# Mask rows of q and k: one ScalarE operation over 128 PSUM rows instead of two over 64, with the sign of q turned

## The chip, the cores and the metric

The kernel runs on one core of a Trainium2 chip. The metric is the device time of one execution in microseconds (us); a version's time is the median of several runs. Five engines work side by side: TensorE (PE), VectorE (DVE), ScalarE (ACT), GpSimd (POOL) and SyncE (SP), which here only issues DMA transfers. Each takes its instructions in a fixed order.

## What is computed

The reference is an attention in which a query sees only the keys of its own cluster, followed by a gated convolution. With B = 4, H = 8, S = 768, D = 64 and 16 centroids for each head:

```python
q_assign = argmax(q_n @ c_n.T)          # cluster of each query, normalised vectors
k_assign = argmax(k_n @ c_n.T)
mask     = q_assign[..., :, None] == k_assign[..., None, :]
scores   = where(mask, q @ k.T / 8, -1e9)
x        = softmax(scores) @ v          # heads side by side: [4, 768, 512]
x1, x2, x3 = split(x @ w_proj, 3)       # w_proj: 512 x 1536
conv     = irfft(rfft(x2, n=768) * rfft(filter_fft, n=768), n=768)   # along the sequence
out      = (x1 * conv * x3) @ w_out     # [4, 768, 512] float32
```

## The kernel before, in words

The work is cut into eight groups n of four heads, half a batch each, and a group into two pairs of heads (pr). The code doesn't issue its work where it stands: `build` describes operations, each with the engines that could do it, what it reads and writes, and a planned time. A table, ORDER, then says for all of them in which order they are issued, on which engine (P, A, V, G, S for the five engines) and in which of the eight PSUM banks. So the order on each engine is that of the table, and an operation that waits holds back what the table put behind it on its engine.

`routing(n)` prepares a group. q and k come into SBUF (`qkraw`, DMAs of L286 on SyncE), are transposed (L560 on VectorE for n of 2 and more) into `qkT` (`qkP` in the trace), and cast to bf16 into `augs` (L249 where ScalarE does it, L251 where GpSimd or VectorE does): 64 rows of q or k for each head of a pair. The similarity to the centroids (L589, TensorE) is turned (L594), its maximum found and compared (L602, L603), and the one-hot choice turned back (`ohT`). One more product (`bank<-ohT,tri` of L71) leaves in a PSUM bank, for 384 positions, 16 rows for each head: those of q on PSUM rows 0 to 63, those of k on rows 64 to 127. Two banks hold the 768 positions. ScalarE brings them to `oh2`, a bf16 view of 64 rows of the tile `sim` with q's and k's 768 values side by side: L612 for q (a copy with scale BIG and bias −BIG), L617 for k (Relu). That makes four operations a routing, 64x384 each, for n = 1 to 7. `masks` (L491) then copies 16 rows for each head with a SyncE DMA into `aug2`, right beside the 64 cast rows, q's and k's 768 values in one transfer: four transfers a routing. The first group (n = 0) has its own way, `first_masks`, which writes the mask rows straight from PSUM (L534 on VectorE, L537 on ScalarE).

`attention(n, pr)` then takes, for each of six key tiles, the scores as a product of 80 or 128 rows (`bank<-aug` of L71), in which the mask rows add nothing for a key of the same cluster and a large negative number for the others. ScalarE exponentiates them with scale 0.125 (L657, L660) into one of five `p` buffers, TensorE multiplies by v (L671, `pair<-p,vraw`), and VectorE (L692) and GpSimd (L688) add up the denominators. Three slots of `augs` go round (`ring`). After each second group the batch's hyena part follows: projection (L809 and others), spectrum (L478), products (L833, L837, L923), output.

The helper `product` (L69, L71) issues most matmuls, and `copy` (L249, L251) most copies and casts, so in the profile these lines stand for several places of the program, and the tile names tell them apart.

Of the kernel before, what the change touches and what calls it, by code (L numbers as in the profile page):

```python
# [14 lines left out]
F32 = mybir.dt.float32  # L15
# [111 lines left out]
P0:7 A30 G12 A43 S42 V16 V31 S44 S41 A45 G25 P1:6 P2:7 P3:6 A34 V49 V50 V32 G29 P4:7 G20 P5:6 P6:7 P7:6 S48 S47 P8:7  # L127
A46 G11 P9:6 P10:7 P70:7 G17 V33 A35 P72:6 S126 S125 V51 G13 G14 G24 A36 A53 V37 P38:5 A71 P66:4 V55 V56 A73 V57 G19
P64:3 A67 V39 P78:4 S124 G28 A65 P76:3 V40 S123 P99:5 V52 A59 A54 V58 V15 G18 A62 A60 A63 P101:6 A102 S130 A100 V21
G61 P146:7 A147 P144:2 P95:1 S129 P93:0 S127 A96 P252:5 V79 A94 P254:7 P151:1 G22 A69 A98 V77 V80 V145 V81 V82 S128  # L130
G23 P88:0 A89 V104 V74 S132 V75 A253 A255 P83:6 V84 S293 V85 A153 S291 P105:2 S122 G154 G68 P107:3 P248:4 P246:5 V90
V108 P148:7 V106 V92 A249 P185:3 A247 A186 P140:4 V141 G103 P264:2 A265 V149 V152 S289 P218:5 A219 P266:4 P192:3
P258:2 A193 S298 A267 G26 G27 G256 P260:5 G97 A259 S136 G250 V87 V91 V86 P212:6 P189:4 A261 V109 A190 P187:3 A188
P194:2 A195 P222:0 A223 S299 V110 A213 V111 P270:15 S290 P117:2 A118 G199 P112:3 A115 P202:0 V150 G200 P196:7 P210:4
A211 P204:6 G139 S295 A197 V272 V271 V273 V274 G135 G201 V121 A203 V113 G138 V275 S294 P206:1 A207 A205 V209 P191:45
A119 P214:0 S292 A120 A116 G134 S297 S133 P226:1 A227 A114 S137 S300 A215 S286 P198 P220:2 A221 P279:6 P228:7 A229
V268 P306:1 A307 P276:3 A277 P304:0 A305 V217 S131 P230:2 A231 V225 P208 P311:1 A312 V317 P309:7 P313:0 G363 V233 A278
A263 P216 V157 V156 A281 S301 S296 S287 S288 A314 P224 A280 S283 S282 V159 P335:3 A257 P302:0 A303 P321:6 A322 P337:1
A310 V316 V433 S245 S464 S465 P232 A234 P235:6 G158 V236 S237 G155 A338 P319:7 A320 A269 P327:0 P323:2 S284 V439 A262
V436 A324 P308:45 S285 P329:7 A251 V430 S460 S461 S468 P331:6 A332 P315 A328 G318 P347:2 A348 V326 V162 P339:1 P325  # L140
P345:2 S471 P371:0 S463 A330 A340 A346 P369:7 A336 A370 V334 A372 A435 V160 V342 S462 P373:6 A374 S458 S238 P343:1
A344 A432 S459 P388:2 P333 A389 P378:0 A379 S362 P442:37 P380:6 V444 A434 S469 P376:1 A377 V350 P341 P398:0 A399 A381
P349 A351 V443 A431 G163 P386:1 P394:0 S473 A387 P352:7 A353 P396:6 A397 P390:3 A391 P406:2 A407 V445 V446 V447 G383
P375:45 P474:7 V719 P414:6 P448:1 A449 G385 S470 S466 A395 A450 A415 P382 A475 S354 P451:2 A453 A452 V239 S240 G368
V716 V384 S467 P412:0 S454 P478:3 A479 V164 S355 P410:1 A411 A413 S242 P392 S241 P404:7 P481:2 S457 S455 V393 A482
V161 V401 A405 P402:6 A403 V409 P400 P166:0 A167 P483:2 A484 P165:7 A169 A171 P503:6 P408 A504 V417 V172 S748 V170
P485:2 A486 P476:1 A477 G489 S745 P416 V356 P142:2 A418 A441 G437 P174:6 V143 S472 P419:1 A420 S357 S421 S422 A175
V168 V243 V244 P495:3 A438 V722 P173:0 A177 V178 P493:2 A494 V176 G364 A440 V725 G365 P491:1 P480:45 P487 P499:2 S456
G488 G490 A496 A492 V498 P515:6 A500 P509:7 P511:3 A510 S358 P501:0 A502 V506 P653:1 A512 P497 V423 P507:0 A654 S747
A508 P664:7 A665 P517:3 A518 A516 P505 P674:7 A675 P672:0 V514 P660:1 P519:3 A520 V522 P657:2 P513 S359 V360 A673  # L150
P678:3 A661 P662:0 S752 V361 S424 A658 A663 S754 S429 P655:7 A656 A721 G667 P728:61 V729 A679 V730 V731 P524:7 S534
S425 V732 P180:0 A525 A717 A720 S526 P521 G669 A523 P670:6 A671 P686:1 A687 V181 V733 V668 S426 P179:7 P682:3 A183
P688:2 A689 V182 S527 V528 S529 P659:45 P666 A683 P734:3 A735 G367 V427 P698:2 A699 P764:7 A765 A736 P676 V677 V428
P680:2 P690:7 S530 A681 V685 P694:3 A695 P696:1 A697 P769:6 P760:2 A761 A691 P684 P737:2 A738 P762:1 A739 S531 A763
V693 G366 A770 A727 P779:3 A780 P692 P700 A702 V701 G703 P793:6 P767:1 A768 V532 P785:3 V533 P777:2 A778 V774 P771:7
A772 G776 S746 V184 A718 P766:45 S744 V886 P535:2 P537:7 A536 V538 P787:0 A786 G775 V539 G704 P781:2 A782 V784 S756
P545:1 P789:3 A546 A790 S759 A788 V792 P540:2 A541 P542:1 V543 S755 P795:0 A796 S753 P547:3 V548 P801:2 A726 P773 V544
P783 S749 A724 S740 S741 P825:1 S758 P844:0 V549 A794 A723 V892 P797:3 A798 A826 P832:6 A833 P803:7 S743 A804 S757
P791 V895 S751 G551 S750 G553 P805:1 G705 S822 S742 V800 P799 P830:7 V889 A806 A802 A845 A890 A831 P842:2 S927 P850:1
P898:60 P834:7 S715 V808 A851 S914 P852:3 A843 V550 S706 G810 P823:1 G552 V900 V899 V901 S915 A853 V902 G838 P807 A824  # L160
P554:1 V555 A809 P827:6 A828 P858:0 V556 A835 G839 P557:3 V558 P578:2 A579 P848:6 A849 P840:7 G811 A859 A841 P829:45
S929 G812 V559 P836 V903 S916 V837 S707 A887 V847 A888 V561 S921 P860:7 P947:3 A861 S924 P930:0 A931 S926 P904:6 A905
S918 A906 P856:1 A857 P868:2 A869 P934:7 A935 P846 P939:6 A940 S917 P907:0 A908 S885 P562:1 A909 V855 P854 A948 S919
V863 V564 V708 P864:6 A865 P565:7 V567 P937:0 A938 V709 A891 P866:2 A867 G560 V563 S920 S911 P593:3 A594 V566 P959:6
P951:0 A952 G569 V871 G873 A897 V568 P862 P870 P932:1 P582:7 V1174 P570:0 A872 V571 A933 V572 P949:3 P973:2 S922 A583
P584:1 V585 P941:7 A942 S813 G945 V1177 A950 P936:45 A974 S710 A960 P573:7 V575 V574 G946 G944 P967:3 A968 V954 P955:0
S923 P963:2 A964 V577 P975:1 A976 A956 P1115:6 P943 P957:1 A958 V962 S925 P953 P965:1 G874 G875 A966 A1176 A1116 S910
P1120:0 P1138:7 P1118:2 A1119 P971:3 P1132:1 S711 P961 A893 P1128:6 A1129 V576 A972 V970 S814 A1121 P969 V978 A896
G980 P586:26 S1209 A587 V589 V588 G590 P1130:3 A1133 P597:0 A894 A1131 S1204 S712 P977 S928 A1179 V1183 S1208 S912
P580:1 V581 P599:6 V1180 P601:23 A1139 A598 V600 G591 A602 V604 V603 P1140:1 A1141 P1136:7 A1137 V815 V816 P595:0 V596  # L170
G592 P1122:1 A1123 S1202 P1146:6 A1147 P1111:7 A1112 P1186:23 G981 V713 V714 P1148:7 A1149 P612:0 P608:6 S913 A979
V1187 V1188 V1189 S876 G1125 V1127 S1203 P1113:7 A613 A1114 V1126 P1220:1 G982 P616:23 V605 S1207 P1154:0 V1135 S817
P1117:45 V1190 S1205 V606 S877 A609 V878 V879 P1152:6 A1153 P1144:7 A1184 S992 S819 P1124 A1178 P1134 A1221 P1142 A617
V619 A1155 A1145 V618 G607 V1191 S818 P1229:0 P614:7 V615 G620 A1230 P1218:3 P1227:2 S1211 A1228 A1219 P1150 P1156:2
A1157 V820 P1237:3 V1143 P1247:7 P1222:0 A1223 S1217 P1192:1 A1193 A1194 P1235:6 A1236 V821 S880 P1158 V1151 P1225:0
S983 P610:1 A1160 A1226 V1234 P1195:6 A1196 V1159 P625:2 S1206 P1224:45 S984 V985 V986 G621 S881 A1197 V611 V622 A1248
A1238 P1243:6 P1245:7 A1244 A1246 S882 V883 S1198 V884 P623:0 A624 V626 P1253:3 A1254 P627:6 S1199 P1263:7 S987 A1264
A628 A1175 P631:01 A632 P1239:3 A1240 G1161 P1261:7 V1347 P1231 G1233 P629:6 V630 P1251:3 A1252 V634 A1262 G1232 S989
P1241 A1181 V633 V1242 S988 S1210 G1162 S1216 G1163 P1255:3 V1250 P1259:7 P1285:1 V990 A1185 P1290:0 V991 A1256 V1258
P1288:6 A1289 A1291 A1260 V635 P1249 P1298:3 A1299 P1283:2 A1284 V1266 G1268 P1316:6 G636 P1257 P1302:7 A1303 P1281:3  # L180
A1282 G637 P1310:0 P1003:2 P993:7 A994 P995:3 V996 S1201 V997 P1000:7 A1311 S1213 P1005:0 A1004 S1212 V1006 V1007
A1286 P998:1 A999 A1182 P1265 A1317 V1001 S1173 G1009 G1008 P1292:0 P1314:1 A1315 P1036:3 A1267 P1040:6 V1350 S1377
P1308:1 A1309 A1041 S1215 A1037 P638:2 V1002 A1293 A639 S1214 V1353 P1051:7 A1052 V1344 V1010 P1055:6 S1164 V1011
# [48 lines left out]
def build(T):  # L232
# [249 lines left out]
    def oh2():  # L482
        return T.sim[:64].rearrange("p a b -> p (a b)").bitcast(BF16).rearrange("p (j s) -> p j s", j=2)
# [59 lines left out]
    def routing(n):  # L543
# [64 lines left out]
        for ch in range(2):  # L608
# [7 lines left out]
            def relu(e, ch=ch, h=h):  # L616
                T.nc.scalar.activation(oh2()[:, 1, ts(ch, 384)], ap(h)[64:, :384], Act.Relu)  # L617
# [342 lines left out]
    def constants():  # L960
# [35 lines left out]
        def small(e):  # L996
            G().memset(T.half_pi, math.pi / 2)
# [227 lines left out]
```

## Time and profile before

| | |
|---|---|
| median of 3 runs | 355.24 us (354.19, 355.83, 355.24) |
| the profiled execution's own time | 353.72 us |
| its span, first to last instruction | 352.0 us |
| granted TensorE clock, mean | 0.997 |
| TensorE busy | 339.8 us, 97% |
| VectorE busy | 324.9 us, 92% |
| ScalarE busy | 275.8 us, 78% |
| GpSimd busy | 155.4 us, 44% |
| evictions to `oh2`, L612 and L617 | 14 each, 0.484 and 0.487 us at the median |
| mask transfers, L491 | 28, issue 0.548 us at the median |

In the profile a row such as `L671 PE MATMUL pair<-p,vraw 128*64 128x385 f32 x768` names the line, the engine, the operation, the tile written and those read, the shape and the number of instructions. SPq and PEq are the sequencers of SyncE and TensorE. An engine's busy time is the union of its instructions' times. A matmul counts from its start to its modelled end, and the next one may start before that. "idle before" is what an engine stood still ahead of the row's operations, with the operation or transfer whose end let it go on.

### The profile page before, as it was taken

What the parts mean: (1) busy time and instruction counts of PE and PEld (TensorE: products, weight loads), DVE (VectorE), ACT (ScalarE), POOL (GpSimd) and SP (SyncE); (2) the same over time, 40 slices, a digit from 0 to 9 for tenths busy, and PEclk for the clock granted to TensorE, in tenths of its full rate; (3) what the DMA queues carried; (4) which work ended last, traced back from release to release, by engine and by line L of the source; (5) the groups of instructions that cost most, each with busy time, mean ns of one, the idle gap of its engine ahead of it and who ended that gap; (6) DMA issues with size and microseconds to landing.
All of it is one profiled execution on the core that took longest, in us unless ns stands there. A gap on an engine that the chain in (4) does not pass through costs nothing.

```text
span 352.0 us, 8375 instructions
## 1 busy us (share of the span) xinstructions
PE 339.8 (97%) x3174; PEld 222.8 (63%) x3176; DVE 324.9 (92%) x452; ACT 275.8 (78%) x513; POOL 155.4 (44%) x175
## 2 busy tenths in 40 slices
PE   7889999999999999999999999999999999999994
PEld 3445445465656568766787577866887865567672
DVE  7999899899999999999989999999988999989993
ACT  5999999999998998887987796869886564534332
POOL 7678405142134545373336638372433054147610
PEclk9999999999999999999999999999999999999998
DMA  8999666875698998998696868983467353310134
GB/s 173 224 161 211 124 103 106 154 153 159 104 175 142 157 173 119 126 124 149 115 194 87 125 80 159 184 161 76 67 141 80 88 156 110 107 61 0 57 126 181
DMA packets 126324, 45.69 MB, mean 130 GB/s; under 512 B 113720, under 2 KB 118604, under 8 KB 126284
## 3 DMA queue, kind: packets, MB, share of 16 engines
q1 hardware_dynamic: 120396, 34.12, 49.0%
q0 software_dynamic: 2960, 9.77, 19.2%
q10 hardware_dynamic: 2928, 1.28, 1.4%
q8 instruction: 25, 0.41, 0.5%
q14 instruction: 15, 0.12, 0.2%
HBM read 31.59 MB, written 7.40 MB: 111 GB/s over the span
## 4 chain that ended last, share of the span: by engine, by line
PE 75%; ACT 3%; DVE 0%; issue 0%; ACTq 0%; DVEq 0%
PE bank L71 38%; PE pair L671 27%; PE bank L809 6%; PE bank L589 2%; PE bank L478 1%; ACT aug L249 1%; ACT p L657 1%; PE bank L705 1%; ACT p L660 0%; PE bank L762 0%; ACT tm L450 0%; PE bank L69 0%; DVE tm L833 0%; ACT tm L249 0%; DVE x L875 0%
## 5 line engine op out<-in xcount | busy, mean ns | idle before, releaser
L671 PE MATMUL pair<-p,vraw 128*64 128x385 f32 x768 | 141.7, 487 | 0.5 <-issue 0.5
L660 ACT ACTIVATE p<-bank 128x512 f32<-128x512 f32 x192 | 108.4, 601 | 27.4 <-PE bank L71 22.1
L692 DVE TENSOR_TENSOR acc<-p,acc 128x1536 f32<-128x1536 f32 x64 | 112.1, 1751 | 4.5 <-ACT p L660 2.1
L71 PE MATMUL bank<-aug 80*64 80x512 bf16 (+3 forms) x746 | 91.7, 330 | 2.3 <-ACT p L660 1.2
L671 PEld LDWEIGHTS pair<-p,vraw 128*64 128x64 f32 x768 | 66.7, 137 | 36.6 <-issue 23.6
L71 PEld LDWEIGHTS <-aug 80*64 80x64 bf16 (+1 forms) x746 | 66.1, 152 | 32.2 <-issue 20.4
L688 POOL TENSOR_TENSOR acc<-p,p 128x512 f32<-128x512 f32 x33 | 42.4, 1312 | 41.9 <-DVE xT L772 22.7
L657 ACT ACTIVATE p<-bank 128x512 f32<-128x512 f32 x96 | 56.2, 602 | 2.9 <-PE bank L71 2.1
L725 POOL DMA_DIRECT2D acc<-acc x30 | 24.4, 814 | 72.9 <-DMA acc<-acc 32.5
L71 PE MATMUL bank<-xT,wpj 128*64 128x384 bf16 x504 | 49.8, 326 | 0.0
L249 ACT CAST aug<-qkP 64x768 bf16<-64x768 f32 x52 | 42.7, 829 | 1.1 <-DVE qkP L560 0.3
L71 PEld LDWEIGHTS <-wpj 128*64 128x64 bf16 x504 | 33.8, 110 | 11.6 <-issue 2.8
L71 PEld LDWEIGHTS <-y 128*64 128x64 bf16 x504 | 27.0, 110 | 10.2 <-issue 2.1
L923 POOL TENSOR_TENSOR y<-yy,x 128x768 bf16<-128x768 f32 x11 | 20.1, 1825 | 24.0 <-DVE yy L911 23.7
L833 DVE TENSOR_TENSOR tm<-bank,hm 128x512 f32<-128x512 f32 x44 | 28.1, 678 | 1.4 <-PE bank L478 0.9
L560 DVE STREAM_TRANSPOSE qkP<-qkraw 128x768 f32<-128x768 f32 x24 | 22.7, 960 | 1.8 <-ACT aug L249 0.9
L71 PE MATMUL bank<-wout,y 128*64 128x512 bf16 (+1 forms) x200 | 23.9, 371 | 0.0
L837 POOL TENSOR_TENSOR y<-tm 128x512 bf16<-128x512 f32 x15 | 19.9, 1352 | 6.7 <-DVE tm L833 2.9
L809 PE MATMUL bank<-wpj,xT 128*64 128x512 bf16 x192 | 22.3, 379 | 0.0
L249 ACT COPY ob<-bank 128x512 f32<-128x512 f32 x20 | 11.6, 587 | 9.4 <-PE bank L71 8.0
L772 DVE SCALAR_TENSOR_TENSOR xT<-osb,rb 128x384 bf16<-128x384 f32 x30 | 17.4, 609 | 0.7 <-DMA rb<-dr 0.7
L809 PEld LDWEIGHTS <-xT 128*64 128x64 bf16 x192 | 13.3, 110 | 6.8 <-issue 0.4
(160 smaller groups left out, 402.9 us busy)
## 6 DMA issues: line engine op xcount, KB each, us to landing
vraw<-in_v_dram SPq DMA_DIRECT2D x16, 384.0 KB
rb<-dr SPq DMA_DIRECT2D x30, 192.0 KB
qkraw<-in_k_dram SPq DMA_DIRECT2D x48, 96.0 KB
qkraw<-in_q_dram SPq DMA_DIRECT2D x48, 96.0 KB
out_dram<-ob SPq DMA_DIRECT2D x9, 512.0 KB
acc<-acc POOLq DMA_DIRECT2D x10, 384.0 KB, 6.1
acc<-acc POOLq DMA_DIRECT2D x10, 192.0 KB, 4.3
wpj<-in_moe_w_proj_dram POOLq DMA_DIRECT2D x4, 384.0 KB, 5.3
```

The costliest lines, as they stand in the source:

```text
L71: T.nc.tensor.matmul(out[64 * i:64 * i + 64], lhsT[:, 64 * i:64 * i + 64], rhs, start=start, stop=stop)
L249: T.nc.scalar.copy(out, in_)
L560: op(("DVE", .9), lambda e, s=s, j=j, pr=pr: V().transpose(T.qkP[pr][:, S * j:S * j + S], T.qkraw[s][:].rearrange("p t h d -> p (t h d)")) ...
L657: T.nc.scalar.activation(o, ap(h).rearrange("p (a b) -> p a b", a=2), Act.Exp, scale=0.125)
L660: T.nc.scalar.activation(flat(s)[:, lo:lo + 512], ap(h), Act.Exp, scale=0.125)
L671: T.nc.tensor.matmul(o[64 * hp:64 * hp + 64, ch, :385], T.vraw[vs][:, hp, sk * D:(sk + 1) * D], T.p[slots[sk]][:, hp, 384 * ch:384 * ch + ...
L688: alu(e).tensor_tensor(o, x, y, op=Alu.add)
L692: T.nc.vector.tensor_tensor(T.acc[os], T.p[slots[sk]][:, :, :S], T.acc[os], op=Alu.add)
L725: op(("POOL", .8), lambda e, rows=rows: T.nc.gpsimd.dma_start(flat_()[:rows], flat_()[rows:2 * rows], accum_op=Alu.add), te, r=[], w=AK, b ...
L809: T.nc.tensor.matmul(ap(h)[64 * i:64 * i + 64], T.xT[xs][:, kt, tokens(m, i, w_)], T.wpj[:, kt, DM:2 * DM], start=kt == 0, stop=kt == ND - 1)
L833: op(("DVE", .68), lambda e, i=i, cs=cs, r=r, h=h: T.nc.vector.tensor_tensor(T.tm[r][:, cs], ap(h), hmrow(i, (0, 2, 2, 3)[2 * r + cs]), op ...
L923: op(("DVE", .95) if last else {"DVE": .95, "POOL": 1.85}, lambda e, dt=dt, x3=x3, yy=yy: alu(e).tensor_tensor(T.y2[:, dt], yy().rearrange ...
```

## The change

For n = 1 to 7 one ScalarE operation now takes all 128 PSUM rows of a bank, q's and k's alike: Relu(scale · x + bias), with scale and bias from a new tile `rank` of one number for each row, 1 and 0 for k's rows and −BIG and BIG for q's. Two operations of 128x384 stand for four of 64x384. Relu leaves only values of zero or more, so q's mask rows come out with the opposite sign (BIG − BIG·x where −BIG + BIG·x was). So the q casts multiply by −1 and the exponential's scale becomes −0.125; the first group's constants are turned to match. `oh2` now keeps q on rows 0 to 63 and k on rows 64 to 127, 768 values each, so a mask transfer takes either q's or k's 16 rows: 56 transfers of 16x768 for 28 of 16x1536. `rank` is filled by four GpSimd memsets near the program's start.

```diff
-P0:7 A30 G12 A43 S42 V16 V31 S44 S41 A45 G25 P1:6 P2:7 P3:6 A34 V49 V50 V32 G29 P4:7 G20 P5:6 P6:7 P7:6 S48 S47 P8:7
+P0:7 A31 G12 A44 S43 V16 V32 S45 S42 A46 G26 P1:6 P2:7 P3:6 A35 V50 V51 V33 G30 P4:7 G21 P5:6 P6:7 P7:6 S49 S48 P8:7
...
     def oh2():
-        return T.sim[:64].rearrange("p a b -> p (a b)").bitcast(BF16).rearrange("p (j s) -> p j s", j=2)
+        return T.sim[:].rearrange("p a b -> p (a b)").bitcast(BF16)[:, :S]
...
-                out.append(op(("SP", .6), lambda e, a=a, hp=hp, lo=lo: dma(e)(
-                    T.aug2[a][hp][64 - 64 * hp:80 - 64 * hp], oh2()[lo:lo + NC]),
...
+                for j in range(2):
+                    out.append(op(("SP", .6), lambda e, a=a, hp=hp, lo=lo, j=j: dma(e)(
+                        T.augs[a][hp][j][64 - 64 * hp:80 - 64 * hp], oh2()[64 * j + lo:64 * j + lo + NC]),
...
-                            T.nc.scalar.activation(o, x, Act.Relu if j else Act.Copy, scale=1.0 if j else BIG,
-                                                   bias=0.0 if j else -BIG)
+                            T.nc.scalar.activation(o, x, Act.Relu if j else Act.Copy, scale=1.0 if j else -BIG,
+                                                   bias=0.0 if j else BIG)
...
+                        if j:
+                            copy(e, o, x)
+                        elif e == "ACT":
+                            T.nc.scalar.activation(o, x, Act.Copy, scale=-1.0)
+                        else:
+                            alu(e).tensor_scalar(o, x, -1.0, None, op0=Alu.mult)
...
-            op(("ACT", .44), lambda e, ch=ch, h=h: T.nc.scalar.activation(
-                oh2()[:, 0, ts(ch, 384)], ap(h)[:64, :384], Act.Copy, scale=BIG, bias=-BIG), due, r=[h],
-               w=[("oh2", 0)] + (SIM if not ch else []), free=[h])
-
-            def relu(e, ch=ch, h=h):
-                T.nc.scalar.activation(oh2()[:, 1, ts(ch, 384)], ap(h)[64:, :384], Act.Relu)
-            op(("ACT", .44), relu, due, r=[h] + ([("oh2", 0)] if not ch else []), w=[("oh2", 1)], free=[h])
+            def ranks(e, ch=ch, h=h):
+                T.nc.scalar.activation(oh2()[:, ts(ch, 384)], ap(h)[:, :384], Act.Relu, scale=T.rank[:, 0:1], bias=T.rank[:, 1:2])
+            op(("ACT", .49), ranks, due, r=[h, "rank"], w=[("oh2", ch)] + (SIM if not ch else []), free=[h])
...
-                        T.nc.scalar.activation(flat(s)[:, lo:lo + 512], ap(h), Act.Exp, scale=0.125)
+                        T.nc.scalar.activation(flat(s)[:, lo:lo + 512], ap(h), Act.Exp, scale=-0.125)
...
+        def rank(e):
+            G().memset(T.rank[:, 0:1], 1.0)
+            G().memset(T.rank[:, 1:2], 0.0)
+            G().memset(T.rank[:64, 0:1], -BIG)
+            G().memset(T.rank[:64, 1:2], BIG)
+        op(("POOL", .4), rank, 7, w=["rank"])
```

ORDER is numbered anew, since there are fewer ScalarE operations and more transfers; the lines above show its first row of both versions. On TensorE, VectorE and GpSimd the remaining operations keep their order. What moves is on ScalarE and SyncE.

On ScalarE at the routing n = 2 (about 58 to 63 us in the trace of before), the first whose evictions stand among exponentials, before: `bank_66` and `bank_67` are the two PSUM banks with the mask rows, `sim` is where `oh2` lies, the `p` tiles are the exponentials' results, `aug` those of the casts.

```order
L660 ACTIVATE p_99<-bank_64 128x512
L612 ACTIVATE sim<-bank_66 64x384
L657 ACTIVATE p_99<-bank_63 128x2x256
L660 ACTIVATE p_98<-bank_65 128x512
L657 ACTIVATE p_100<-bank_64 128x2x256
L617 ACTIVATE sim<-bank_66 64x384
L249 CAST aug_93<-qkP_109 64x768
L617 ACTIVATE sim<-bank_67 64x384
L660 ACTIVATE p_100<-bank_63 128x512
L612 ACTIVATE sim<-bank_67 64x384
L249 CAST aug_97<-qkP_108 64x768
```

And the same place after the change, with the rows' new line numbers.

```order
L665 ACTIVATE p_99<-bank_64 128x512
L662 ACTIVATE p_99<-bank_63 128x2x256
L665 ACTIVATE p_98<-bank_65 128x512
L662 ACTIVATE p_100<-bank_64 128x2x256
L622 ACTIVATE sim<-bank_66,rank 128x384
L582 ACTIVATE aug_93<-qkP_109 64x768
L622 ACTIVATE sim<-bank_67,rank 128x384
L665 ACTIVATE p_100<-bank_63 128x512
L250 CAST aug_97<-qkP_108 64x768
```

The first bank's eviction stands where the second of its two stood, the second bank's where the first of its two stood; the other two are gone. The q cast (`aug_93`) has become an operation with a scale.

On SyncE the mask transfers of one routing (n = 3, about 100 to 108 us in the trace of before) among the loads of q, k and v, before; `aug` are the `augs` tiles, `qkraw` and `vraw` the loaded q, k and v.

```order
L286 DMA qkraw_86<-in_k_dram 32x24x32
L491 DMA aug_92<-sim 16x1536
L491 DMA aug_93<-sim 16x1536
L286 DMA qkraw_88<-in_k_dram 32x24x32
L491 DMA aug_95<-sim 16x1536
L286 DMA qkraw_88<-in_k_dram 32x24x32
L286 DMA qkraw_86<-in_k_dram 32x24x32 x2
L301 DMA vraw_90<-in_v_dram 128x2x384
```

And after.

```order
L287 DMA qkraw_86<-in_k_dram 32x24x32
L493 DMA aug_92<-sim 16x768 x2
L493 DMA aug_93<-sim 16x768 x2
L287 DMA qkraw_88<-in_k_dram 32x24x32
L493 DMA aug_95<-sim 16x768 x2
L287 DMA qkraw_88<-in_k_dram 32x24x32
L287 DMA qkraw_86<-in_k_dram 32x24x32 x2
L302 DMA vraw_90<-in_v_dram 128x2x384
```

Each mask transfer has become two, one directly behind the other, and the loads behind them on the queue keep their places.

More of the change, by code (lines that the diff above doesn't have):

```diff
@@ L132 @@
[L132 to L146, printed above, removed]
@@ L1162 @@
     T.osb = [tl([128, 2, 385], F32, f"osb{i}") for i in range(3)]
+    T.rank = tl([128, 2], F32, "rank")
     T.dn, T.rb, T.dp = tl([128, 12], F32, "dn"), tl([128, S], F32, "rb"), tl([128, ROWS + 1, 12], F32, "dp")
```

205 lines of the change are left out of this document (111 added, 94 removed).

## The prediction

> **What bounds the kernel now.** I read the page first, then the busy time of each engine by stretches, then TensorE's groups in the stretch that stood out, then the timelines of ScalarE, SyncE and VectorE around the changed operations.
>
> ```profile
> PE 339.8 (97%) x3174; PEld 222.8 (63%) x3176; DVE 324.9 (92%) x452; ACT 275.8 (78%) x513; POOL 155.4 (44%) x175
> ```
>
> By this row TensorE is the bound, and ScalarE, where the change removes work, has a fifth of the span to spare. That is an average over stages. The view by stretches (start and end, length, then busy time of PE, PEld, DVE, ACT and POOL, granted clock, DMA share, GB/s) separates them:
>
> ```profile
> 32.00:100.00 68.00, 66.61 (x536) 36.69 (x535) 62.93 (x69) 66.64 (x123) 21.23 (x20) 1.00 0.73 136
> 100.00:140.00 40.00, 40.00 (x350) 26.65 (x348) 39.49 (x48) 36.49 (x66) 19.99 (x19) 1.00 1.01 152
> 140.00:260.00 120.00, 119.54 (x1151) 86.33 (x1149) 114.69 (x149) 100.71 (x187) 56.21 (x52) 1.00 0.78 130
> ```
>
> From 32 to 100 us ScalarE is busy 66.64 of 68 us and TensorE 66.61: they go in lockstep, and the busy row lets TensorE gain only 1.39 us there. From 100 on TensorE has no idle time worth naming (0.46 us in 160), and to 140 VectorE has only 0.51 us left.
>
> But the busy time of pipelined matmuls overstates: each has its latency counted beside the next one's streaming. So I count what TensorE had to stream from 32 to 100 us, with its groups of that stretch (columns: form, count, busy, mean ns, idle before):
>
> ```profile
> L671 PE MATMUL pair<-p,vraw 128*64 128x385 f32 x228 | 41.8, 487 | 0.0
> L71 PE MATMUL bank<-aug 80*64 80x512 bf16 x58 | 11.1, 387 | 0.5 <-ACT sim L612 0.2 <-ACT p L657 0.2
> L71 PE MATMUL bank<-aug 128*64 128x512 bf16 x51 | 9.8, 382 | 0.3 <-ACT p L657 0.2
> L71 PE MATMUL bank<-aug 80*64 80x256 bf16 x52 | 7.6, 275 | 0.5 <-ACT p L660 0.4
> L71 PE MATMUL bank<-aug 128*64 128x256 bf16 x52 | 7.6, 273 | 0.0
> L705 PE MATMUL bank<-acc,ones 128*32 128x384 f32 x32 | 3.4, 494 | 0.1
> L589 PE MATMUL bank<-qkP,cbd 128*32 128x384 f32 x32 | 3.0, 492 | 0.0
> ```
>
> and with rates from the chain that ended last, where these matmuls stand back to back:
>
> ```profile
> 153.29 1.43 PE bank L589 x16
> ...
> 179.68 1.30 PE pair L671 x8
> ...
> 263.67 4.32 PE bank L809 x40
> ```
>
> One matmul of L671 streams in 1.30/8 = 0.161 us, one 512 wide in 4.32/40 = 0.108, one 256 wide in half of that, one of L589's kind in 1.43/16 = 0.089. So 228 × 0.161 = 36.8, 109 × 0.108 = 11.8, 104 × 0.054 = 5.6, 64 × 0.089 = 5.7, and at most 0.108 for each of the other 31 of 536: 3.3. Together 63.2 of 68 us: about 4.8 us were lost in this stretch, though 1.39 show as idle. One such place in TensorE's timeline:
>
> ```profile
> 97.79 0.68 PE L71 MATMUL bank<-aug 80*64 80x512 bf16 x4
> 98.66 0.90 PE L71 MATMUL bank<-aug 80*64 80x512 bf16 x6 [0.19 <-ACT p L657]
> ```
>
> The first four need 4 × 0.108 = 0.43 us and the next group starts 0.87 us after them: 0.44 lost, 0.19 counted. [...]
>
> **The evictions.** Each of seven routings (n = 1 to 7) now has two ScalarE operations where it had four. The second routing in ScalarE's timeline:
>
> ```profile
> 58.78 0.50 ACT L612 ACTIVATE sim<-bank 64x384 bf16<-64x384 f32 x1
> 59.15 0.61 ACT L660 ACTIVATE p<-bank 128x512 f32<-128x512 f32 x1
> 59.78 0.49 ACT L617 ACTIVATE sim<-bank 64x384 bf16<-64x384 f32 x1
> 60.30 1.08 ACT L660 ACTIVATE p<-bank 128x512 f32<-128x512 f32 x2
> 61.41 0.49 ACT L617 ACTIVATE sim<-bank 64x384 bf16<-64x384 f32 x1
> 61.90 0.48 ACT L612 ACTIVATE sim<-bank 64x384 bf16<-64x384 f32 x1
> 62.29 1.06 ACT L660 ACTIVATE p<-bank 128x512 f32<-128x512 f32 x2
> ```
>
> From 58.78 to 62.29 are 3.51 us with four evictions and three exponentials. Two exponentials in a row take 1.08, and each of them alone 0.60, so one after another costs 0.49. Three cost 1.47, and the four evictions 3.51 − 1.47 = 2.04 us.
>
> No row has the new operation: 128 rows, with scale and bias from a tile. Its bounds come from these rows (the first three give an operation's least, median and greatest ns; the last is the group on the page):
>
> ```profile
> L366 ACT ACTIVATE fw<-ob,half_pi x2: 609/610/612, 9.8 to 10.6; 128x384 bf16<-128x384 f32 x2
> L364 ACT ACTIVATE fw<-tm x2: 507/522/536, 6.2 to 9.4; 128x384 bf16<-128x384 f32 x2
> L450 ACT ACTIVATE tm<-bank,hw x6: 677/692/702, 65.2 to 88.2; 128x512 f32<-128x512 f32 x6
> ...
> L660 ACT ACTIVATE p<-bank 128x512 f32<-128x512 f32 x192 | 108.4, 601 | 27.4 <-PE bank L71 22.1
> ```
>
> An eviction of 64 rows takes 0.49, L364's 128 rows of the same length 0.522, so twice the rows cost 0.03 at most, and I count them at nothing. A bias from a tile costs 0.610 − 0.522 = 0.09, a scale from a tile 0.692 − 0.601 = 0.09. Both together are in no row: between 0 (hidden) and 0.18. I take 0.18, since each row shows its own operand at full price: 0.67 us for one operation. Two of them, less 0.1 where the next one overlaps, are 1.24, so a routing saves 2.04 − 1.24 = 0.80 us of ScalarE (1.17 if the operands were free). The page "ScalarE: Activation LUTs" of the Trainium skill, section on what a table load costs, adds about 93 ns for each pointer operand; an estimate by its figures is 0.69 us for one operation and 0.76 saved.
>
> What reaches the end: routings 4 to 7 stand behind 100 us, where TensorE is full; their 3.2 us become ScalarE's idle time and count nothing. Routings 1 and 2 (about 32–37 and 58–62 us) stand where ScalarE is the bound: 2 × 0.8 = 1.6. The third is split. Its last two evictions lie on the chain that ended last before 100 us:
>
> ```profile
> 95.04 0.25 ACT sim L612
> ...
> 95.54 0.49 ACT sim L617
> ```
>
> There 0.49 goes and the other grows by 0.18: 0.3 us. Its first one stands by TensorE's work of 90–92 us, where the chain is TensorE's; nothing is counted for it. Sum: **1.9 us earlier** at 100 us.
>
> **The mask transfers.** SyncE issues 56 of half the size where it issued 28. Its timeline (issue by issue; four pieces between 100 and 108 us) beside VectorE's, at the busiest place, then the nearest row for a transfer's landing:
>
> ```profile
> 100.74 2.74 SPq L491 DMA_DIRECT2D aug<-sim  x2
> 103.53 0.78 SPq L286 DMA_DIRECT2D qkraw<-in_k_dram  x1
> 104.40 0.97 SPq L491 DMA_DIRECT2D aug<-sim  x1
> 105.42 1.79 SPq L286 DMA_DIRECT2D qkraw<-in_k_dram  x3
> ```
>
> ```profile
> 109.90 1.84 DVE L560 STREAM_TRANSPOSE qkP<-qkraw 128x768 f32<-128x768 f32 x2
> ```
>
> ```profile
> 0.81 0.45 ACTq L306 DMA_DIRECT2D sd<-in_centroids_dram  x1
> ```
>
> ```profile
> 3.26 0.22 DVE L309 TENSOR_TENSOR sd<-sd 128x64 f32<-128x64 f32 x1 [0.98 <-DMA sd<-in_centroids_dram]
> ```
>
> ```profile
> L491 SPq DMA_DIRECT2D aug<-sim x28: 512/548/1985, 37.3 to 255.3; - x28
> ```
>
> An issue takes 0.55 us at the median: 28 × 0.55 = 15 us more on SyncE, spread over 218 us. At most places SyncE waits longer than that. Here three mask issues stand ahead of the loads at 105.42, so those leave 3 × 0.55 = 1.65 us later. The second transpose of the 109.90 pair starts near 110.8 and reads what the last of the three loads, issued by 107.2, brings: 3.6 us of lead. The centroids' load ended its issue at 1.26 and was used at 3.26: 2.0 us to land. The slack is 1.6 against a delay of 1.65. VectorE, full there, may then wait 0 to 1 us; I take 0.3, since masks and loads also move 1.9 us earlier with the rest. This is **0.3 us back**.
>
> The masks themselves are complete at most four issues (2.2 us) later in each routing. Whether scores then wait is read from TensorE's waits, where this is the one row with a transfer (total, times, longest):
>
> ```profile
> PE bank L568 <- DMA qkraw<-in_q_dram: 0.7, 1, 0.7
> ```
>
> It belongs to the loads at the start; no score has ever waited for a mask. How much room there is the row doesn't tell: nothing counted, up to 0.5 us against it.
>
> **The sign of q.** The q casts become a multiplication by −1. On ScalarE it is the same operation with a scale in the instruction, which L612's evictions have too (0.49 for 384, like L617's without): 0 each. On VectorE one cast late in the program, where it has idle time: 0. On GpSimd five:
>
> ```profile
> 15.53 1.59 POOL L251 CAST aug<-qkP 64x768 bf16<-64x768 f32 x2
> ...
> 22.33 2.52 POOL L688 TENSOR_TENSOR acc<-p,p 128x512 f32<-128x512 f32 x2 [1.55 <-ACT p L660]
> ```
>
> A cast of 768 takes 0.8 there; the nearest dearer row has two inputs and takes 1.26 for 512, so 1.9 for 768. I take 0.8, the row with one input and one output as here. At 1.9 the first score matmuls of the program, which need the cast of 15.53, would come 1.1 us later, and the 1.55 us of idle time ahead of 22.33 would cover the four others. GpSimd's four writes of scale and bias, of one column each, come in its first microseconds, long before the first routing's 32 us: nothing. The exponential's new scale and the swapped constants of the first group cost nothing.
>
> **Sum.** 1.9 − 0.3 = 1.6 us. The profiled execution took 353.72 us (1.72 around its span of 352.0), and would take 352.1. The median of the three runs, 355.24, is 1.52 above it; I carry the difference over: **353.6 us**. What a measurement can tell from no change is about 0.5%, 1.8 us, so the forecast lies just inside it.
>
> **Rivals.**
>
> *A, the gain is lost on the way.* TensorE's busy row is right, or VectorE, with 0.51 us idle from 100 to 140 us, is what is late next. Then 0 to 0.8 us remain: 354.4 to 355.2. For it: VectorE's 39.49 of 40. Against it: VectorE has 5 us idle from 32 to 100, so its work moves forward with the rest, and the 0.44 us lost at 98.66 are behind ScalarE, not VectorE. Chance 0.18.
>
> *B, SyncE becomes the bound, and it is slower.* Two mask issues at 100.74 took 2.74 us, 1.4 each, with the DMA engines' share at 1.01 from 100 to 140 us. If a mask issue takes 1.4 instead of 0.55 in such bursts, three more are 4.1 us against a slack of 1.6: VectorE, full, waits 2.5 us there, and about 1 us in one later routing: 3.5 − 1.9 = 1.6 us slower, 356.8. It decides from about 1.2 us per issue, where the wait at 110 us alone (3 × 1.2 − 1.6 = 2.0) eats the 1.9. Against it: the median of 28 issues is 0.55, and most of that 2.74 us may be a wait within SyncE's own queue. Chance 0.14, slower than before; somewhat over half of it by more than 1.8 us.
>
> *C, the operation is as dear as the two it replaces.* From 1.07 us each (2 × 1.07 − 0.1 = 2.04) nothing is saved: 355.2 less or more the 0.3. The rows give 0.67, so only an operand from a tile on 128 PSUM rows with a price of its own would do it. Chance 0.05.
>
> *D, more than counted.* The operands are free (1.17 a routing), and the third routing counts in full: 3.5 us, 351.7. [...] Chance 0.08.
>
> **How the numbers follow.** The forecast's own case, with 0.8 to 2.4 us gained (352.8 to 354.4), has the remaining 0.55. For 8 in 10 the range goes from 352.3, which takes in the nearer half of D, to 355.6, which takes in all of the forecast's case, of A and of C, and a little of B. Faster by over 1.8 us: D, and the two fifths of the forecast's case below 353.4, with some of the spread of three runs: 0.33. Slower by over 1.8 us: most of B, 0.09. The rest, 0.58, is within.
>
> **What would show it.** Right: 14 operations of 128x384 with a mean of 0.58 to 0.69; ScalarE's busy time lower by 5 to 8 us; the matmuls that stand at 98.66 come 1.5 to 2 us earlier, and the idle places of TensorE put down to ScalarE before 100 us shrink; 56 mask issues near 0.55. Wrong: the same matmuls not earlier (A, or C with a mean above 1 us), or VectorE waiting for loads of q and k by DMA near 110 us and later (B), or GpSimd's products with −1 far above 0.8 us and TensorE's first scores later.

## The result, and the profile after

The changed kernel takes 359.06 us (median of 22 runs, 356.16 to 361.4) where the kernel before takes 355.28 (22 runs): a ratio of 1.0102, 95% interval 1.0076 to 1.0128. It is 1.0% slower, 3.6 to 3.8 us. The forecast was 353.6, with 352.3 to 355.6 as its range.

The profiled execution of the changed kernel took 360.33 us, its span is 358.5. Its busy times, and then the same stretches as before (columns as there):

```profile
PE 341.5 (95%) x3174; PEld 226.2 (63%) x3176; DVE 326.1 (91%) x452; ACT 272.4 (76%) x499; POOL 162.2 (45%) x179
```

```profile
32.00:100.00 68.00, 66.32 (x543) 36.07 (x542) 64.27 (x70) 66.16 (x119) 24.97 (x21) 1.00 0.68 131
100.00:140.00 40.00, 38.29 (x321) 25.94 (x319) 35.59 (x42) 33.77 (x60) 16.14 (x15) 1.00 0.96 148
140.00:260.00 120.00, 117.80 (x1136) 85.43 (x1133) 114.19 (x151) 97.38 (x177) 59.93 (x54) 1.00 0.80 127
```

ScalarE has lost 3.4 us of work (the prediction named 5 to 8 as a sign of being right) and GpSimd has gained 6.8. Between 100 and 140 us, where TensorE was full and VectorE had 0.51 us left, TensorE now idles 1.7 us and VectorE 4.4. Something made both wait.

To see where the time went I counted ScalarE's 288 exponentials through in each trace. Their order is the same in all kernels, so the start of the nth can be compared. The table gives, for single executions, how much later the nth starts than in the kernel before (us; the left column is the start in the kernel before). The other columns are the experiments below: e8 is the changed kernel a second time, e2, e3, e10 and e11 are the kernel before with one part of the change, the rest the changed kernel with a part or two altered.

| n, start before | after | e8 | e1 | e2 | e3 | e4 | e5 | e6 | e10 | e11 | e12 |
|---|---|---|---|---|---|---|---|---|---|---|---|
| 0, 18.51 | 1.47 | 0.51 | −0.06 | 1.84 | 0.90 | 0.41 | 1.56 | 0.95 | 1.65 | 0.00 | 0.21 |
| 16, 31.46 | 3.26 | 2.37 | −0.06 | 4.70 | 0.90 | 3.29 | 1.88 | 1.86 | 4.50 | 0.00 | 1.26 |
| 96, 99.68 | 2.12 | 1.22 | −1.25 | 4.87 | 0.90 | 2.11 | 0.73 | 0.76 | 4.48 | 0.30 | 0.13 |
| 120, 121.28 | 5.70 | 3.64 | −0.11 | 5.01 | 1.69 | 2.78 | 0.82 | 1.66 | 4.53 | 0.47 | 0.53 |
| 224, 229.15 | 4.99 | 3.90 | 1.56 | 5.00 | 1.72 | 1.95 | 0.03 | 1.83 | 4.50 | 0.98 | 0.52 |
| 240, 247.69 | 7.18 | 5.04 | 1.36 | 6.31 | 1.74 | 3.09 | −0.21 | 1.61 | 4.50 | 2.31 | 0.29 |
| 287, 301.38 | 7.16 | 5.02 | 1.34 | 6.31 | 1.74 | 3.08 | −0.22 | 1.59 | 4.49 | 2.31 | 0.27 |

In the column "after" there are three losses and one gain: 1.8 us lost from n = 0 to 16 (3.26 − 1.47), 1.1 gained to n = 96, 3.6 lost around 100 to 121 us, 2.2 lost around 229 to 248. The 1.5 us at n = 0 is at least in part the start of this one execution: e5, e3 and e11, whose early casts on GpSimd are those of the kernel before, have 1.56, 0.90 and 0.00. Over the first 10 us the granted clock was 0.86 in this execution, 0.85 in e3's and 1.00 in e11's.

**The first and the third loss are GpSimd's.** Its multiplication in its timeline, and then all five with those who waited (total us, times):

```profile
16.99 2.13 POOL L584 TENSOR_SCALAR aug<-qkP 64x768 bf16<-64x768 f32 x1
...
22.00 4.24 POOL L584 TENSOR_SCALAR aug<-qkP 64x768 bf16<-64x768 f32 x2
```

```profile
L584 POOL TENSOR_SCALAR aug<-qkP x5: 2135/2138/2143, 17.0 to 232.5; 64x768 bf16<-64x768 f32 x5
...
  DVE qkP L562: 2.5, 2
  ACT qkP L250: 1.8, 1
```

It takes 2.14 us where the cast took 0.82. Those who wait in this trace don't read the result. They write the next q and k into `qkP`, which GpSimd is still reading. ScalarE's copy waits, and TensorE waits for that:

```profile
24.17 0.86 ACT L250 COPY qkP<-bank 128x384 f32<-128x384 f32 x2 [1.84 <-POOL aug L584]
```

```profile
24.70 0.38 PE L69 MATMUL bank<-aug 80*128 80x256 bf16 x2 [1.37 <-ACT qkP L250]
```

The same again at 232 us, where VectorE's transpose into `qkP` waits; the last row is the same transpose in the kernel before, behind the cast:

```profile
232.52 2.13 POOL L584 TENSOR_SCALAR aug<-qkP 64x768 bf16<-64x768 f32 x1
```

```profile
234.69 0.98 DVE L562 STREAM_TRANSPOSE qkP<-qkraw 128x768 f32<-128x768 f32 x1 [1.70 <-POOL aug L584]
```

```profile
228.16 0.98 DVE L560 STREAM_TRANSPOSE qkP<-qkraw 128x768 f32<-128x768 f32 x1 [0.36 <-POOL aug L251]
```

That wait is 1.34 us longer, and e8, e2 and e11 lose 1.1 to 1.3 us at this place. The other 0.9 us of the 2.2 is in the one execution of the column "after" alone.

**The second loss is SyncE's.** The queue at 106 us, and VectorE's wait for a load of k:

```profile
106.06 4.31 SPq L493 DMA_DIRECT2D aug<-sim  x4
110.42 1.32 SPq L287 DMA_DIRECT2D qkraw<-in_k_dram  x1
111.84 1.74 SPq L493 DMA_DIRECT2D aug<-sim  x2
113.62 1.72 SPq L287 DMA_DIRECT2D qkraw<-in_k_dram  x3
```

```profile
116.46 0.98 DVE L562 STREAM_TRANSPOSE qkP<-qkraw 128x768 f32<-128x768 f32 x1 [1.81 <-DMA qkraw<-in_k_dram]
```

The three loads leave 8.2 us later than in the kernel before (113.62 against 105.42), while the work around them is some 2 to 4 us later. VectorE's wait ends with the first of the three. The chain of work that ended last runs through the queue there (start, us, what):

```profile
109.79 0.59 SPq L493
...
110.42 1.32 SPq L287
...
111.84 1.10 SPq L493
...
112.99 0.59 SPq L493
...
113.62 2.82 DMA qkraw<-in_k_dram
...
116.46 0.98 DVE qkP L562
```

So the loads stand behind the issues themselves, one after the other. Three of the issues ahead of them are new, at 0.59 us each, and single ones are long: from 102.76 on they are 2.33 (a load of q), 2.41 (the first mask), 1.32 and 1.10 us. In the kernel before the longest there is 1.99 us, part of the prediction's row of 2.74. What makes a single issue long isn't shown.

**The gain is ScalarE's.** The new operation costs what was taken for it:

```profile
L622 ACT ACTIVATE sim<-bank,rank x14: 666/674/704, 37.5 to 250.1; 128x384 bf16<-128x384 f32 x14
```

### The profile page after: what moved, and what is told of

Same layout as the page of the kernel before. It is cut to its first block, busy times and chain, and to the rows that moved or that the text cites. A ratio compares the mean times of both kernels' runs of the same rounds, so it can differ in the third digit from the quotient of the medians.

```text
span 358.5 us, 8421 instructions
## 1 busy us (share of the span) xinstructions
PE 341.5 (95%) x3174; PEld 226.2 (63%) x3176; DVE 326.1 (91%) x452; ACT 272.4 (76%) x499; POOL 162.2 (45%) x179
## 4 chain that ended last, share of the span: by engine, by line
PE 75%; ACT 6%; POOL 6%; DVE 5%; issue 3%; DMA 2%; SPq 1%; DVEq 0%; POOLq 0%; ACTq 0%
PE bank L71 36%; PE pair L676 28%; PE bank L814 6%; DMA qkraw<-in_k_dram 2%; POOL aug L584 2%; ACT p L665 2%; PE bank L598 2%; PE bank L479 1%; DVE acc L697 1%; ACT p L662 1%; PE bank L710 1%; POOL acc L693 1%; DVE qkP L562 1%; ACT aug L250 1%; ACT aug L582 1%
## 5 line engine op out<-in xcount | busy, mean ns | idle before, releaser
L71 PE MATMUL bank<-aug 80*64 80x512 bf16 (+3 forms) x746 | 90.7, 329 | 3.3 <-ACT p L665 1.4
L676 PEld LDWEIGHTS pair<-p,vraw 128*64 128x64 f32 x768 | 68.1, 137 | 35.8 <-issue 21.3
L250 ACT CAST aug<-qkP 64x768 bf16<-64x768 f32 x26 | 21.4, 827 | 2.2 <-DVE qkP L562 1.8
L582 ACT ACTIVATE aug<-qkP 64x768 bf16<-64x768 f32 x26 | 21.8, 841 | 0.4
```

Source lines behind the costliest of these rows:

```text
L71: T.nc.tensor.matmul(out[64 * i:64 * i + 64], lhsT[:, 64 * i:64 * i + 64], rhs, start=start, stop=stop)
L250: T.nc.scalar.copy(out, in_)
L582: T.nc.scalar.activation(o, x, Act.Copy, scale=-1.0)
L676: T.nc.tensor.matmul(o[64 * hp:64 * hp + 64, ch, :385], T.vraw[vs][:, hp, sk * D:(sk + 1) * D], T.p[slots[sk]][:, hp, 384 * ch:384 * ch + ...
```

## The experiments

Two theories of the loss stood against each other: G, GpSimd's multiplication; Q, the doubled mask issues on SyncE. Each kernel ran in turn with the kernel before on the same chip. A measured time stands against the median of those runs of the kernel before; the ratio is to them too, but isn't simply the quotient of the two medians.

**e1_pool_casts**, the changed kernel with GpSimd's q casts left as they were:

```diff
-                        if j:
+                        if j or e == "POOL":
                             copy(e, o, x)
```

> The changed kernel, but GpSimd's five q casts stay plain casts (the sign of these five heads' q is left out). Theory G, GpSimd's multiplication is the cost (2.14 us in the changed kernel's trace where the cast took 0.82, three times before 27 us and once at 232.5 us on the chain): about 3.9 us come back, 1.8 before 32 us and 2.1 near 230 us, time about 355.2. Theory Q, SyncE's doubled mask issues are the cost (3.6 us lost between 100 and 115 us): the time stays within 1 us of the changed kernel's 359.1.

Measured: 355.72 us against 354.60, ratio 1.0040 (1.0011 to 1.0070). Some 60% of the loss is gone, 0.62% or 2.2 us. So G is right that the multiplication costs most of it; 3.9 us were foretold, which is too much, and something is left. In the table both of GpSimd's losses are gone from its column. A new one of 1.7 us stands between n = 120 and 224; in the chain there two mask issues come first, then the transfer of a sum that waits behind them:

```profile
131.31 0.32 SPq L493
131.63 0.04 issue
131.67 0.66 SPq L493
...
133.13 2.73 DMA dd<-acc
```

e3 and e6, which issue as many masks, lose only 0.03 and 0.17 us there. So this loss isn't shown to belong to the masks.

**e2_before_pool_mul**, the kernel before with GpSimd's q casts alone multiplied by 1.0:

```diff
-                       lambda e, a=ring(n, pr), hp=hp, j=j, z=z: copy(
-                        e, T.augs[a][hp][j][64 * hp:64 * hp + 64],
+                       lambda e, a=ring(n, pr), hp=hp, j=j, z=z: (
+                        (lambda o, x: T.nc.gpsimd.tensor_scalar(o, x, 1.0, None, op0=Alu.mult)) if e == "POOL" and not j else
+                        (lambda o, x: copy(e, o, x)))(
+                        T.augs[a][hp][j][64 * hp:64 * hp + 64],
```

> The kernel before with GpSimd's five q casts alone made a multiplication (by 1.0, so the result is the same). Theory G: 1.8 us later by 32 us and up to 2.1 near 230 us, so 357.1 to 359.2 against 355.3. Theory Q: 355.3, within 0.5.

Measured: 359.10 against 354.60, ratio 1.0122 (1.0079 to 1.0165). It lies within what G foretold. This one part alone makes the kernel as slow as the whole change.

**e3_before_split**, the kernel before with each mask transfer cut in two:

```diff
-                out.append(op(("SP", .6), lambda e, a=a, hp=hp, lo=lo: dma(e)(
-                    T.aug2[a][hp][64 - 64 * hp:80 - 64 * hp], oh2()[lo:lo + NC]),
+                out.append(op(("SP", .6), lambda e, a=a, hp=hp, lo=lo: [dma(e)(
+                    T.augs[a][hp][j][64 - 64 * hp:80 - 64 * hp], oh2()[lo:lo + NC, j]) for j in range(2)],
```

> The kernel before with each mask transfer alone cut in two halves of 16x768, 56 issues for 28. Theory Q: VectorE waits for loads of k near 110 us, up to 3.6 us are lost, 356.5 to 358.9. Theory G: 355.3, within 0.5.

Measured: 356.25 against 354.60, ratio 1.0060 (1.0031 to 1.0088). Q holds too, at 1.6 us by the medians and 2.1 by the ratio: both theories are right, each for a part. Of this the table's column shows 0.8 us around 100 to 121 us, and 0.9 us at the start that belongs to its one execution; where the rest falls in other executions isn't shown.

**e4_28_masks**, the changed kernel with one mask transfer for two:

```diff
-                    ... j=j: dma(e)(T.augs[a][hp][j][64 - 64 * hp:80 - 64 * hp], oh2()[64 * j + lo:64 * j + lo + NC]),
+                    ... j=j: j or dma(e)(T.aug2[a][hp][64 - 64 * hp:80 - 64 * hp],
+                        oh2()[64 + lo:64 + lo + NC].unsqueeze(1).to_broadcast([NC, 2, S])),
```

> The changed kernel with one mask transfer where it has two, 28 issues of the old size (k's mask rows are brought to q's place as well, so q's mask rows are left out). Theory Q: the 3.6 us between 100 and 115 us come back, about 355.5. Theory G: the time stays within 1 us of 359.1.

Measured: 356.37 against 354.60, ratio 1.0049 (1.0021 to 1.0076): 1.9 us back. Around 100 to 121 us it loses 0.7 us where the changed kernel lost 3.6.

What holds the loads back can be told from SyncE's issues in the traces. The transfers of SyncE use eight semaphores in turn, so an issue may have to wait until the transfer eight issues earlier, which has the same semaphore, has landed. In e1 one such wait is on its chain (start, us, what):

```profile
99.14 7.21 DMA qkraw<-in_k_dram
106.35 0.02 issue
106.36 4.27 DMA qkraw<-in_k_dram
110.63 0.02 issue
110.65 0.98 DVE qkP L562
```

The load at 106.36 is issued 0.01 us after the one of 99.14 has landed; between them stand one other load and six mask issues. But the issue before it had ended only 0.14 us earlier, so this wait held the queue for 0.1 us at most. In the changed kernel's trace the load of 113.62 has its eighth predecessor at 105.14, and that had landed by 109.80: no wait at all. So it is the issues that delay the loads. From the issue of the q loads ahead of the masks (98.75 in the kernel before) to that of the three loads of k are 6.7 us in the kernel before, 8.5 in e1, 8.2 in e3 and in e6, but 11.5 in the changed kernel and 10.9 in e8. The three more issues account for the 1.5 to 1.9 us that e1, e3 and e6 have more (an issue takes 0.588 us at the median in the changed kernel, 0.548 before). The further 2.4 to 3.3 us of the changed kernel are long single issues.

**e5_evictions_only**, e1's and e4's edits together:

> The two earlier edits together: GpSimd's q casts stay plain (the sign of five heads' q is left out) and one mask transfer stands where the changed kernel has two (q's mask rows are left out, k's brought twice). What is left of the change is the eviction in one operation and the signs on ScalarE and VectorE. If the prediction's sum for the evictions holds (0.8 us of ScalarE a routing, three routings count) the time is 1.5 to 2 us below before, about 352.8 to 353.3 where before is 354.6. If TensorE or VectorE swallow it (rival A), it is within 0.8 us of before.

Measured: 354.40 against 354.91, ratio 0.9978 (0.9950 to 1.0006). By the medians 0.5 us are gained and by the ratio 0.8, not clear of no change, where 1.5 to 2 were foretold. In the table it gains 2.1 us from n = 16 to the end (1.88 to −0.22), behind a start that was 1.6 us late. So one execution's trace shows a gain of the size forecast, but the times don't confirm it.

**e6_sign_on_k**, the whole change without GpSimd's multiplication:

```diff
-                        if j:
+                        if not n or j != (casts[key, 0].on == "POOL"):
                             copy(e, o, x)
...
-scale=-0.125)
+scale=-0.125 if n else 0.125)
```

(The first group's constants go back, and one q cast of GpSimd's and one k cast of VectorE's change engines in ORDER.)

> The whole change, but with no multiplication on GpSimd: the first group keeps its old signs, and in the later groups the sign is put on k where GpSimd casts q (one of the early casts changes place with VectorE). 56 mask transfers stay. Theory G: 3.3 us below the changed kernel, as with the plain casts: about 355.7, 1 us above before, which is what the doubled mask issues leave. Rival: the cost was not the multiplication but GpSimd's order; then the time stays near 359.

Measured: 355.65 against 354.91, ratio 1.0015 (0.9982 to 1.0049): 0.7 us above before, near what was foretold, and not to be told from it. With e1 and e2, which leave GpSimd's order as it was, this says that the multiplication was the cost and not the order. What is left isn't the masks alone, as the expectation had it. The early q cast that VectorE has taken over stands ahead of three of its mask evictions, and TensorE waits for them (0.45 us in the kernel before):

```profile
20.33 0.89 DVE L584 TENSOR_SCALAR aug<-qkP 64x768 bf16<-64x768 f32 x1
```

```profile
22.91 1.26 PE L69 MATMUL bank<-aug 80*128 80x256 bf16 x8 [1.35 <-DVE aug L536]
```

The 0.9 us by which this wait is longer is what e6 loses from n = 0 to 16 in the table; e12 loses 1.05 there in the same way.

**e7_sign_k_masks_pool**, e6 with half of the masks of two routings issued by GpSimd:

```diff
-lambda e, a=a, hp=hp, lo=lo, j=j: dma(e)(
+lambda e, a=a, hp=hp, lo=lo, j=j: (T.nc.gpsimd.dma_start if j and n in (3, 4) else dma(e))(
```

> As e6_sign_on_k, and in the two routings at 100 to 113 and near 131 us k's mask transfers are issued by GpSimd, so SyncE's queue there is as short as before. Theory Q for the rest (SyncE's issues hold back loads and the denominators' transfers): 1 to 2.5 us below e6_sign_on_k, about 353.5 to 354.5, at or just below before. Rival: GpSimd waits for the evictions and holds back its own sums, or the transfers and not their issue are what is late: no gain, or slower than e6_sign_on_k.

Measured: 374.91, ratio 1.0564 (1.0508 to 1.0620). A miss; the rival came true, at 20 us: the transfers, issued by GpSimd, come later still. TensorE's wait and GpSimd's timeline:

```profile
PE bank L71 <- DMA aug<-sim: 13.9, 3, 8.3
```

```profile
144.06 0.77 POOL L730 DMA_DIRECT2D acc<-acc  x1 [1.83 <-DMA acc<-acc]
149.33 0.77 POOL L730 DMA_DIRECT2D acc<-acc  x1 [4.50 <-DMA aug<-sim]
149.85 0.76 POOL L493 DMA_DIRECT2D aug<-sim  x1
```

GpSimd issues its own accumulations as transfers one behind the other and waits for each, and the masks stand between them.

**e8_after_again**, the changed kernel itself:

> The changed kernel itself, unchanged, beside the three others on one chip: 358 to 360, 1.0% above before. If the lower clock at the start of its profiled execution belongs to the change, nearly all its executions have it; if it is chance, the share is like that of the other kernels.

Measured: 358.51 against 354.91, ratio 1.0090 (1.0060 to 1.0119). Its profiled execution had a clock of 1.00 throughout, and lost at the same places: 1.9, 2.4 and 1.1 us, with 1.15 gained. So the lower clock at the start of the first profile doesn't come with the change each time. In 6 of its 12 executions the mean granted clock was 0.991 or less, in the kernel before beside it in 4 of 29; the last section comes back to that.

**e9_loads_first**, e6 with two pairs of mask transfers behind loads in ORDER:

```diff
-... S743 S744 S745 S746 P832:1 S765 ... S749 S750 A811 S764 P798 V902 S758 G556 S757 ...
+... S743 S744 P832:1 S765 S745 S746 ... A811 S764 P798 V902 S758 G556 S757 S749 S750 ...
```

> As e6_sign_on_k, and on SyncE near 104 to 112 us the loads of k that VectorE waits for go ahead of two pairs of mask transfers. Theory Q: the loads leave about 1 us earlier and the 0.9 us lost between 100 and 115 us come back: 0.5 to 1 us below e6_sign_on_k, at about the time before. Rival: the masks, now later, hold back TensorE's scores instead: no gain.

Measured: 358.84 against 354.56, ratio 1.0128 (1.0081 to 1.0174). A miss: one score (P832) stood directly behind its masks in ORDER, so it was now taken before them, with what the slot held, and the masks had to wait for it on SyncE, with everything behind them:

```profile
SPq L493 <- PE bank L71: 5.2, 1, 5.2
```

The prediction left open how much room the scores have behind their masks; at this place the order has none.

**e10_early_mul** and **e11_late_mul**, e2 for the three early casts alone and for the two late ones alone:

```diff
-if e == "POOL" and not j
+if e == "POOL" and not j and n < 2      (e10; n > 1 in e11)
```

> The kernel before with the three early q casts of GpSimd (before 27 us) alone made multiplications by 1.0. Theory G: about 2 to 3 us later, 357 to 358 where before is 355, with a lower granted clock before 32 us in a good part of the executions, as in the other kernels with these three. Rival: the late one is what costs, then within 0.5 us of before.

> The kernel before with the two late q casts of GpSimd (near 60 and 230 us) alone made multiplications by 1.0. Theory G: 1.1 to 1.3 us later from the one near 230 us, where VectorE's transposes wait for it, nothing from the one near 60 us: about 356.2 where before is 355. Rival: hidden, within 0.3 us of before.

Measured: 358.13 against 354.56, ratio 1.0085 (1.0056 to 1.0115), and 356.05, ratio 1.0048 (1.0025 to 1.0070). Both places cost: 3.0 and 1.7 us by the ratios. In the table e11 loses 1.3 us from n = 224 to 240, as foretold, and 1.0 us in small steps before that, more than foretold.

**e12_loads_first_2**, e6 with only the second of e9's moves:

> As e6_sign_on_k, with only one pair of mask transfers (the one that no score near it needs) moved behind the three loads of k on SyncE, so the loads leave about 1.1 us earlier; no score is taken before its masks, as one was in e9_loads_first. Theory Q: of the 0.9 us lost between 100 and 115 us about half comes back, 0.3 to 0.6 us below e6_sign_on_k, at or just below before. Rival: the wait is for the transfers eight issues earlier and not for the two issues moved; no gain.

Measured: 354.61 against 355.49, ratio 0.9980 (0.9950 to 1.0011). The queue now:

```profile
103.01 2.87 SPq L493 DMA_DIRECT2D aug<-sim  x4
105.93 2.29 SPq L287 DMA_DIRECT2D qkraw<-in_k_dram  x4
108.31 2.41 SPq L493 DMA_DIRECT2D aug<-sim  x2
```

The last three loads leave by 108.2 us, where in e6, 0.6 us later in all, they left between 108.3 and 111.3, and the loss between n = 96 and 120 is 0.4 us (0.9 in e6). This version has the whole change, with the sign on k where GpSimd casts q, and by the ratios is 1.2% below the changed kernel; it stands 0.2% below the kernel before, which the interval doesn't tell from no change.

## Why the prediction was wrong

The sum was 1.9 − 0.3. Term by term, with what the runs showed:

- **GpSimd's multiplication: the step that failed.** The prediction put it so: "I take 0.8, as" the row "with one input and one output as here", with 1.9 as the other end. It is 2.14, above both. The dear end's price (1.1 us at the first scores) was worked out, but entered neither the sum nor any rival's chance. And the waits that were considered were those of the result's readers and of GpSimd's own next operations. In the changed kernel's trace the two who waited were writers of the operand, ScalarE's copies and VectorE's transposes into `qkP`. In the traces of e2 and e10 the first score, a reader, waited as well, 0.89 and 0.97 us, so that half of the thought was not wrong. The term was 0; by the ratios it measured 3.0 us for the early three (e10), 1.7 for the late two (e11), and 4.3 for all five (e2). The page "GPSIMD Engine Reference" of the Trainium skill, section "Engine selection", calls one-input operations on GpSimd roughly line-rate. The traces bear that out for the cast, more or less (0.82 us on GpSimd, 0.56 on VectorE), and not for the multiplication by a constant (2.14 and 0.56).
- **The mask transfers: the right place, too small.** 0.3 was taken, up to 1 bounded. Alone it is 2.1 us by e3's ratio (0.8 of it in its trace at the place named), 1.9 by e4's beside the changed kernel's. VectorE's wait at that place is 0.5 us in e3, 0.9 in e1 and 0.4 in e6, within the bound, but 1.81 in the changed kernel. The delay was well taken: 1.65 us for three more issues, 1.5 to 1.9 measured in e1, e3 and e6. The slack was right by luck. The transpose reads the first of the three loads and not the last, and such a load lands 2.8 to 4.3 us after its issue begins (in the changed kernel and e1), not 2.0 us after its end; in the trace of before it had landed 1.9 us ahead of the transpose, where 1.6 was worked out. What the forecast had no term for is the long single issues of the changed kernel. Rival B had this place, VectorE's wait and the sign. Its mechanism, issues of 1.4 us in a burst, is not the rule (the median stayed at 0.588), but single issues of 1.1 to 2.4 us did delay the loads here.
- **The evictions: right for one operation, not confirmed at the end.** One operation costs 0.674, taken 0.67. In e1's second routing two of them take 1.11 us with what they push aside, where 2.04 stood:

```profile
58.92 0.69 ACT L622 ACTIVATE sim<-bank,rank 128x384 bf16<-128x384 f32 x1
59.47 1.09 ACT L665 ACTIVATE p<-bank 128x512 f32<-128x512 f32 x2
60.42 0.70 ACT L622 ACTIVATE sim<-bank,rank 128x384 bf16<-128x384 f32 x1
60.98 1.10 ACT L665 ACTIVATE p<-bank 128x512 f32<-128x512 f32 x2
```

  Each is followed 0.55 us later by the next. That is 0.93 saved, 0.8 forecast. But by n = 96 only 1.1 to 1.2 us are gained in each of the table's seven kernels that have it (3.26 − 2.12, 2.37 − 1.22, and so on along the rows 16 and 96), not 1.9. A further 0.9 comes behind that in e5 (0.73 at n = 96 to −0.21 at 240), where nothing was counted. The prediction found 4.8 us of TensorE's time lost before 100 us (4.5, with 1.30/8 = 0.1625 in place of its 0.161) where 1.39 show as idle. The 1.1 to 1.2 us stay below both and decide nothing between them. Rival A (the gain is swallowed) did not hold in e5's trace; its median and ratio, 0.5 and 0.8 us, leave it open.
- **The sign on ScalarE and VectorE: right.** 0.841 against 0.828 us at the median on ScalarE, 0.557 in both on VectorE.
- **The parts taken together.** Alone, the multiplication costs 1.22%, the masks 0.60%, and e5 gains 0.22%: 1.60%, and the change measures 1.02%. The intervals of the three (0.43, 0.29 and 0.28 to either side) are wide enough for the difference to be noise. At 100 to 121 us the traces point the other way: 3.6 and 2.4 us were lost there with both (after and e8), 1.1 and 0.7 with either (e1, e4). Why single issues grow long when both are there is not settled.

## What to carry to other kernels

A cast that is given a constant to multiply by cost 2.6 times as much on one engine (GpSimd, 2.14 us for 0.82) and nothing on another (VectorE, 0.557 in both). So price such an operation with a row of the same operation on the same engine, and if there is none, give the dear end a chance of its own. Ask for each longer operation who writes next what it reads, not only who reads what it writes. And a transfer cut in two is issued twice, and the loads behind it on the queue pay for that.

## What was not expected of the hardware

TensorE's clock can fall behind such a wait. In e4's profiled execution the same wait behind GpSimd was 1.55 us long, and the matmuls behind it ran at half the clock (stretches as above, the clock is the third column from the right):

```profile
23.71 1.01 PE L69 MATMUL bank<-aug 80*128 80x256 bf16 x3 [1.55 <-ACT qkP L250]
24.65 2.58 PE L599 MATMUL bank<-qkP,cbd 128*32 128x384 f32 x16
```

```profile
22.00:24.00 2.00, 0.45 (x4) 0.23 (x2) 1.71 (x3) 0.82 (x3) 2.00 (x2) 0.87 0.95 195
24.00:26.00 2.00, 2.00 (x15) 0.49 (x17) 0.00 (x0) 2.00 (x6) 2.00 (x2) 0.50 0.74 111
26.00:28.00 2.00, 2.00 (x22) 0.67 (x16) 0.62 (x2) 0.95 (x3) 1.82 (x3) 0.78 0.89 165
```

The 16 similarity products took 2.58 us instead of 1.5. In the profiles of e2 and e10 the wait is 1.55 us too and the clock falls to 0.50 as well. But in e8's profile the wait is the same 1.55 us, the clock stays at 1.00, and the products take 1.50:

```profile
23.81 0.60 PE L69 MATMUL bank<-aug 80*128 80x256 bf16 x3 [1.55 <-ACT qkP L250]
24.34 1.50 PE L598 MATMUL bank<-qkP,cbd 128*32 128x384 f32 x16
```

In the first profile of the changed kernel the wait is 1.37 us and the clock stays at 1.00 there. From n = 0 to 16 the table has 2.9 us lost in e2, e4 and e10, and 1.8 and 1.9 in the changed kernel's two columns: about 1 us is the clock's. It comes by chance: it falls in some executions and not in others.

Over all runs the mean granted clock was 0.991 or less in 23 of 58 executions of the five kernels with the three early multiplications (after, e8, e2, e4, e10), and in 2 of 72 of the six without them and with no other long added wait (e1, e3, e5, e6, e11, e12). But it was so in 12 of 92 executions of the kernel before that ran beside the experiments. And the mean doesn't say where the clock fell: e2 and e10, at 0.989 and 0.990, had it low both in the first 16 us and behind the wait, e4, at 0.994, behind the wait alone. So the counts fit a clock that falls more often with the multiplications, and don't measure it. Among executions at 0.997 or more, the changed kernel in e8 is 2.7 us above the kernel before (medians of 4 and 14: 356.94 and 354.25), among all 3.6: most of the loss is not the clock's.

The page "TensorE: Matmul & The Clock Gate" of the Trainium skill, section "What's actually happening", has the clock halve after an idle window of about 3.4 us that runs free of the kernel. The halving and its coming by chance agree with these traces; the length doesn't, since here a wait of 1.55 us among short matmuls was enough in three of four traces.
